# Block-diagonal K and V operands for windowed attention, inside a kernel rewritten around one precomputed order

## The chip, the cores and the metric

The kernel runs on one core of a Trainium2 chip. The metric is device time in microseconds (us) of one execution, as the median of several. On one core an execution is called slow when it is over 1.5% above the fastest of the same kernel; times below are of fast runs unless a sentence says otherwise. "PE" is the tensor engine, "PEld" its weight loads, "DVE" the vector engine, "ACT" the scalar engine, "POOL" GpSimd, and "SP" the engine that here does little else than issue DMAs.

## The reference

Two independent computations share one launch, and their outputs stand side by side.

```python
# (a) S4 convolution: L = 2048 steps, D = 1024 channels, N = 128 states
K = jnp.einsum("dn,dnl,dn->dl", Cc, exp(dt * A * l), dt * Bc).real   # the filter
y = irfft(rfft(u padded to 4096) * rfft(K padded))[:2048] + u * Dskip

# (b) attention, 32 heads of 32, each query sees 8 keys: itself and every
#     second position before it (dilation 2)
q, k, v = x @ wqkv
idx = pos[:, None] - (arange(8) * 2)[None, :]        # masked where negative
o = softmax(q . k[idx] / sqrt(32)) . v[idx]
return concatenate([y, o @ wo], axis=-1)
```

## The kernel before

The first part of the kernel (up to 271 us in its trace) makes Q, K and V by matrix products and, woven in between, the convolution filter with 2048 tiny matmuls. The second part runs the convolution as FFT stages by matmul, and the attention. Even and odd positions are split, so that the dilated window becomes 8 neighbours; queries and keys go in blocks of 32. Four heads of 32 rows share the 128 partitions.

Attention loads whole rows for 256 queries (`ru`) with three DMAs, and multiplies with four packed 32x32 tiles of the array per key block, one for each head:

```python
    def loads(self, ru):
        ...
        nc.sync.dma_start(out=qs[:], in_=self.qv[:, :, q0:q0 + RU])
        nc.sync.dma_start(out=ks[:, :, 32 * f:], in_=self.kv[:, :, q0 - 32 + 32 * f:q0 + RU])
        nc.sync.dma_start(out=vs[:, f:, :], in_=self.Vd[:, b0 - 1 + f:b0 + 8, :])

    # scores of one group of four heads (ct): 9 key blocks x 4 heads
    for b in range(-1, NB):
        ...
        for h in range(4):
            hs = slice(32 * h, 32 * h + 32)
            nc.tensor.matmul(S[hs, o:o + n], lhsT=ks[hs, ct, kb:kb + 32], rhs=qs[hs, ct, qa:qa + n],
                             start=True, stop=True, tile_position=(32 * h, 32 * h), ...)
```

Two generators, convolution and attention, are interleaved by a fixed ratio. The convolution sends its intermediate results (`Zu`, `Zk`, `Zv`) through DRAM to change their layout, and multiplies the two spectra straight from PSUM:

```python
    # step 1, for u and for the filter k
    self.bal.copy(zs[:, 2 * rp:2 * rp + 2, :], pz[:], 1024)
    ...
    nc.sync.dma_start(out=Z[:, n2:n2 + 4, :], in_=zs[64 * b:64 * b + 64])
    # middle
    nc.gpsimd.dma_start(out=t[64 * ri:64 * ri + 64], in_=self.Z[n][hf]...)
    V.tensor_tensor(out=pr[:, x], in0=F[1][:], in1=kf[...], op=ALU.mult)     # F[1] in PSUM, f32

    drive(conv(), 64 + 36 + 16, at.gen(), 80)
```

The softmax here doesn't subtract the row's maximum and nothing guards it: scores larger than these inputs give would overflow.

## Time and profile before

| | before |
|---|---|
| median of 3 runs | 691.88 us (686.53 to 692.02) |
| span of the profiled run | 688.6 us, mean granted PE clock 0.846 |
| PE / DVE / ACT / POOL busy | 70% / 55% / 54% / 15% |
| first part, 0 to 271 us | PE bound from 92 us on |
| second part, 271 to 688.6 us | no engine bound; waits on loads, on order, on instruction supply |

A page of the profile gives busy times over the whole span, then the span in 40 slices (busy tenths of each engine, granted PE clock in tenths, DMA share), the DMA queues, the chain of work that ended last, the costliest groups of instructions, and the DMA issues. The prediction below shows most of what matters. Two lines that it does not show are needed later. They are from the page of the kernel before, the granted clock by slice and the line of the queue that SP fills (packets, MB, share of the 16 DMA engines' time):

```profile
PEclk9997999999999898655885955687997997699979
...
q1 hardware_dynamic: 95376, 88.63, 49.3%
```

The clock falls in the middle of the span, where PE waits; and SP's queue moves 88.63 MB with 95376 packets, 929 bytes each on average.

### The profile page before, as it was taken

How to read it: one execution, taken by the hardware profiler on the slowest of the kernel's cores; microseconds unless marked ns; L12 is line 12 of the kernel's file. 1: busy time of each engine (PE TensorE's matmuls, PEld its weight loads, DVE VectorE, ACT ScalarE, POOL GpSimd, SP SyncE). 2: the span in 40 equal slices, each digit the busy share in tenths (PEclk: the TensorE clock that was granted, in tenths of full speed). 3: DMA queues.
4: the chain of work that ended last, by engine and by line, in shares of the span. 5: the costliest groups of instructions: out<-in, count | busy, mean ns of one | idle time of the engine just before them, and what ended most of it. 6: DMA issues, size and time to landing. Idle time of an engine off the chain costs nothing.

```text
span 688.6 us, 23065 instructions
## 1 busy us (share of the span) xinstructions
PE 484.9 (70%) x10268; PEld 247.5 (36%) x10268; DVE 376.1 (55%) x595; ACT 369.0 (54%) x608; POOL 105.4 (15%) x163
## 2 busy tenths in 40 slices
PE   0284989899999785303775962569788885779866
PEld 0031546556556455102343431224332341223432
DVE  4758878768777802221544431245855862576442
ACT  3585798698798623102554432334646752656441
POOL 5400111010110000000010020000545644350000
PEclk9997999999999898655885955687997997699979
DMA  9980322132231164999585699375997899894685
GB/s 145 258 165 16 93 79 92 59 102 72 79 103 66 54 223 136 255 181 253 136 272 177 199 224 178 91 231 145 328 270 199 243 218 253 220 264 99 185 223 161
DMA packets 103891, 116.19 MB, mean 169 GB/s; under 512 B 46992, under 2 KB 84112, under 8 KB 102128
## 3 DMA queue, kind: packets, MB, share of 16 engines
q1 hardware_dynamic: 95376, 88.63, 49.3%
q0 software_dynamic: 8416, 26.10, 13.9%
q8 instruction: 80, 1.31, 0.8%
q14 instruction: 19, 0.16, 0.1%
HBM read 58.59 MB, written 50.33 MB: 158 GB/s over the span
## 4 chain that ended last, share of the span: by engine, by line
PE 35%; DVE 15%; DMA 15%; ACT 14%; issue 10%; SPq 3%; POOL 0%; ACTq 0%; DVEq 0%
PE cp L579 6%; PE ps L383 6%; DMA Zv<-vs 4%; PE psv L399 4%; DMA big<-Zv 4%; PE cp L627 3%; DVE OR L195 3%; PE O L566 3%; PE S L550 2%; PE pk L239 2%; PE cp L653 2%; DVE OL L224 2%; PE cp L669 2%; DVE OL L223 2%; DMA Kd<-K 2%
## 5 line engine op out<-in xcount | busy, mean ns | idle before, releaser
L383 PE MATMUL ps<-xT,w 128*128 128x512 bf16 x512 | 129.7, 403 | 53.7 <-DMA xT<-in_B_x_dram 32.8
L659 DVE TENSOR_TENSOR pr<-cp,kf 128x1024 bf16<-128x1024 f32 x64 | 75.7, 1219 | 42.7 <-ACT kf L499 33.5
L383 PEld LDWEIGHTS <-w 128*128 128x128 bf16 x512 | 49.1, 102 | 119.1 <-issue 61.9
L550 PE MATMUL S<-qs,ks 32*32 32x40 bf16 (+2 forms) x2304 | 38.9, 185 | 60.3 <-ACT pe L553 20.9
L579 PE MATMUL cp<-wosb,oT 128*128 128x512 bf16 x256 | 62.4, 397 | 4.7 <-ACT zs L499 2.8
L570 ACT ACTIVATE ln<-O 128x256 f32<-128x256 f32 x64 | 24.6, 384 | 73.2 <-PE O L566 66.3
L643 POOL DMA_DIRECT2D zk<-Zk x64 | 38.2, 600 | 164.3 <-PE S L550 82.9
L399 PE MATMUL psv<-wv,xT 128*32 128x256 bf16 x2048 | 62.2, 273 | 0.0
L550 PEld LDWEIGHTS <-ks 32*32 32x32 bf16 x2304 | 27.5, 96 | 93.7 <-issue 72.9
L643 POOL DMA_DIRECT2D zu<-Zu x64 | 38.1, 600 | 138.9 <-PE S L550 117.3
L572 DVE TENSOR_TENSOR oT<-O,ln 128x256 bf16<-128x256 f32 x64 | 27.0, 422 | 54.4 <-ACT ln L571 54.4
L627 PE MATMUL cp<-big,l 128*128 128x512 bf16 x128 | 43.2, 450 | 18.2 <-DMA big<-in_A_u_dram 12.9
L399 PEld LDWEIGHTS <-xT 128*32 128x32 bf16 x2048 | 52.5, 97 | 7.2 <-issue 6.4
L499 ACT CAST vs<-cp 128x1024 bf16<-128x1024 f32 x32 | 32.4, 1012 | 39.8 <-DMA Zv<-vs 26.3
L502 DVE CAST zs<-cp 128x1024 bf16<-128x1024 f32 x36 | 43.0, 1218 | 17.5 <-PE cp L627 17.4
L553 ACT ACTIVATE pe<-S 128x320 bf16<-128x320 f32 x64 | 27.7, 433 | 43.3 <-PE S L550 42.3
L554 DVE TENSOR_TENSOR pm<-pe,mk 128x320 bf16<-128x320 bf16 x64 | 20.3, 320 | 50.8 <-ACT pe L553 32.4
L669 PE MATMUL cp<-pr,m 64*128 64x512 bf16 x256 | 41.2, 423 | 7.7 <-ACT vs L499 5.5
L499 ACT CAST zs<-cp 128x1024 bf16<-128x1024 f32 x28 | 28.0, 1009 | 34.2 <-PE cp L627 22.1
L182 DVE TENSOR_SCALAR PA<-PH 128x1024 int32<-128x1024 int32 (+1 forms) x36 | 27.9, 775 | 27.2 <-ACT TL L186 19.4
L579 PEld LDWEIGHTS <-oT 128*128 128x128 bf16 x256 | 25.2, 102 | 37.2 <-issue 11.8
L653 PE MATMUL cp<-zu,m 128*64 128x512 bf16 x128 | 24.0, 437 | 20.0 <-ACT vs L499 13.2
(105 smaller groups left out, 750.2 us busy)
## 6 DMA issues: line engine op xcount, KB each, us to landing
Zu<-zs SPq DMA_DIRECT2D x32, 256.0 KB, 5.1
Zk<-zs SPq DMA_DIRECT2D x32, 256.0 KB, 5.5
zu<-Zu POOLq DMA_DIRECT2D x64, 128.0 KB, 6.3
zk<-Zk POOLq DMA_DIRECT2D x64, 128.0 KB, 6.1
Zv<-vs SPq DMA_DIRECT2D x64, 128.0 KB, 3.9
big<-Zv SPq DMA_DIRECT2D x16, 512.0 KB, 7.6
w<-in_B_wqkv_dram POOLq DMA_DIRECT2D x16, 256.0 KB, 4.9
QT<-sg SPq DMA_DIRECT2D x16, 256.0 KB, 2.1
```

The costliest lines, as they stand in the source:

```text
L182: V.tensor_scalar(out=PA[:, 0:n, :], in0=PH[:, 0:n, :], scalar1=16384.0, scalar2=None, op0=ALU.add)
L383: nc.tensor.matmul(ps[:, h, :], lhsT=self.w[ct][:, kt, t, :], rhs=self.xT[:, kt, t0:t0 + 512], start=(kt == 0), stop=(kt == 7))
L399: nc.tensor.matmul(ps[32 * h:32 * h + 32, b * 256:b * 256 + 256].rearrange("p (c d) -> p c d", d=32), lhsT=self.xT[:, kt, t0:t0 + 32], rhs ...
L499: self.nc.scalar.copy(out=out, in_=in_)
L502: self.nc.vector.tensor_copy(out=out, in_=in_)
L550: nc.tensor.matmul(S[hs, o:o + n], lhsT=ks[hs, ct, kb:kb + 32], rhs=qs[hs, ct, qa:qa + n], start=True, stop=True, tile_position=(32 * h, 3 ...
L579: nc.tensor.matmul(po[:, h, :], lhsT=oT[:, ct, tt * 128:(tt + 1) * 128], rhs=self.wo[:, ct, h * 512:(h + 1) * 512], start=(ct == 0), stop= ...
L627: nc.tensor.matmul(pz[:, i, :], lhsT=self.l1[:, mt, :], rhs=src[:, rq * 4 + rp * 2 + i, :], start=True, stop=True)
L643: nc.gpsimd.dma_start(out=t[64 * ri:64 * ri + 64], in_=self.Z[n][hf][4 * p + ri:4 * p + 4:2].rearrange("ab n d -> n ab d"))
L653: nc.tensor.matmul(f[64 * ab:64 * ab + 64, ri, :], lhsT=w[:, ab, 64 * ri:64 * ri + 64], rhs=z[:, ab, :], start=True, stop=True, tile_posit ...
L659: V.tensor_tensor(out=pr[:, x], in0=F[1][:], in1=kf[:, x:x + 1, :].to_broadcast([128, 2, 512]), op=ALU.mult)
L669: nc.tensor.matmul(v[:, ab, :], lhsT=w[rs, t, :], rhs=pr[rs, x, y, :], start=(i == 0), stop=(i == 3), tile_position=(64 * ab, 0), skip_gro ...
```

## The change

The title names block-diagonal operands. Instead of four packed 32x32 matmuls, K of four heads stands as four 32x32 blocks on the diagonal of a 128x128 operand whose other elements are zero, and one full-array matmul does all four heads; the same for V. The zeros are written once into three sets of operands. The price is that a load must place each head's blocks separately. The diff is much larger than that, though: nearly the whole kernel is rewritten.

- All work is cut into tasks, and one precomputed order, stored as a table, fixes the sequence on every engine, SP and POOL included. Stage boundaries go.
- DMA transposes of x and of the parameters become plain loads and 176 PE transposes.
- `Zu`, `Zk` and `Kd` no longer go through DRAM; u is reordered inside DRAM by 16 DMAs with runs of 128 B.
- V is made by full-array matmuls. Both spectra are copied to SBUF as bf16 before the product.

```diff
-    def loads(self, ru):
-        nc.sync.dma_start(out=qs[:], in_=self.qv[:, :, q0:q0 + RU])
-        nc.sync.dma_start(out=ks[:, :, 32 * f:], in_=self.kv[...])
-        nc.sync.dma_start(out=vs[:, f:, :], in_=self.Vd[:, b0 - 1 + f:b0 + 8, :])
+        self.kb = [cst.tile([128, 2, 9, 128], BF, name=f"kb{i}") for i in range(3)]
+        self.vb = [cst.tile([128, 9, 2, 128], BF, name=f"vb{i}") for i in range(3)]
+    def load(self, ru, qt, i, st):                      # 32 times: 8 ru x 4 qt
+        nc.sync.dma_start(out=st["q"][:], in_=self.QT[ru][:, 2 * qt:2 * qt + 2, :])
+        for h in range(4):
+            hs = slice(32 * h, 32 * h + 32)
+            nc.sync.dma_start(out=self.kb[i][hs, :, :, hs]..., in_=self.KT_[ru][hs, 2 * qt:2 * qt + 2, :]...)
+        for h in range(4):
+            hs = slice(32 * h, 32 * h + 32)
+            for c in range(2):
+                nc.sync.dma_start(out=self.vb[i][hs, f:, c, hs], in_=self.Vd[hs, b0 - 1 + f:b0 + 8, 64 * qt + 32 * c:64 * qt + 32 * c + 32])
 ...
-                    for h in range(4):
-                        nc.tensor.matmul(S[hs, o:o + n], lhsT=ks[hs, ct, kb:kb + 32], rhs=qs[hs, ct, qa:qa + n], ..., tile_position=(32 * h, 32 * h))
+            nc.tensor.matmul(S[:, o:o + n], lhsT=st["k"][:, ct % 2, kb, :], rhs=st["q"][:, ct % 2, qa:qa + n], ...)
 ...
+            nc.vector.memset(self.kb[i][:], 0.0); nc.vector.memset(self.vb[i][:], 0.0)
 ...
+                    ld = P("SP", 3.2, ... self.load(ru, ct // 2, i, st) ...)     # 3.2: the task list's own figure for a load
 ...
-    drive(conv(), 64 + 36 + 16, at.gen(), 80)
+        seq = plan.order()                               # a table of 1864 entries, decoded from text
+        for t in seq:
+            t.fn(t.pick)
```

## The prediction

> **What bounds the kernel now.** I read the page's engine totals and slices first, then the busy time by stretch, then the waits of the tensor engine, the groups, the chain and the DMA queue's issues.
>
> ```profile
> span 688.6 us, 23065 instructions
> PE 484.9 (70%) x10268; PEld 247.5 (36%) x10268; DVE 376.1 (55%) x595; ACT 369.0 (54%) x608; POOL 105.4 (15%) x163
> ...
> 0.00:27.00 27.00, 0.00 (x0) 0.10 (x1) 13.86 (x29) 14.80 (x23) 12.71 (x20) 1.00 1.04 203
> 27.00:92.00 65.00, 44.94 (x396) 20.85 (x396) 51.58 (x69) 43.92 (x66) 8.43 (x6) 0.92 0.49 109
> 92.00:271.00 179.00, 163.20 (x4226) 100.89 (x4226) 118.26 (x219) 134.10 (x223) 8.21 (x10) 0.96 0.27 89
> 271.00:318.00 47.00, 10.55 (x206) 5.35 (x205) 14.11 (x39) 6.71 (x11) 0.00 (x0) 0.58 1.01 220
> 318.00:490.00 172.00, 114.95 (x2908) 57.58 (x2909) 71.38 (x114) 70.51 (x142) 9.50 (x16) 0.71 0.71 195
> 490.00:640.00 150.00, 118.41 (x1845) 46.83 (x1845) 88.24 (x102) 82.84 (x118) 66.53 (x112) 0.87 0.87 230
> 640.00:688.60 48.60, 32.85 (x688) 15.89 (x686) 18.71 (x27) 16.08 (x31) 0.00 (x0) 0.89 0.67 191
> ```
>
> In each stretch the columns are length, busy PE, weight load, DVE, ACT and POOL, then granted clock, DMA share, GB/s. No engine bounds the whole. Up to 271 us is the first half (QKV projection and generation of the convolution filter), the rest is convolution and attention. Only one stretch, 92 to 271, is bound by PE (163 of 179 us). Before 27 us PE does nothing, from 27 to 92 it is busy 45 of 65; from 271 to 318 DMA is full and PE is all but idle; after that everything is half used, at a reduced clock. The waits and chain say on what:
>
> ```profile
> PE ps L383 <- DMA xT<-in_B_x_dram: 32.8, 8, 27.0
> PE ps L383 <- ACT sg L386: 13.2, 5, 9.9
> ...
> PE S L550 <- ACT pe L553: 20.9, 28, 1.1
> PE S L550 <- issue: 19.9, 7, 6.6
> PE S L550 <- DMA ks<-KT: 19.2, 2, 15.8
> PE cp L653 <- ACT vs L499: 13.2, 9, 4.5
> PE cp L627 <- DMA big<-in_A_u_dram: 12.9, 1, 12.9
> ...
> PE 35%; DVE 15%; DMA 15%; ACT 14%; issue 10%; SPq 3%; POOL 0%; ACTq 0%; DVEq 0%
> ```
>
> The first matmul waits 27 us for the DMA transposes of x. Later the fixed order of the two interleaved generators makes PE stand before scores whose single PSUM buffer is still being read (ACT pe), before loads, and for its own instructions (issue). The chain changes hands everywhere: this is a latency and ordering problem, so a better order can gain much.
>
> ```profile
> L659 DVE TENSOR_TENSOR pr<-cp,kf 128x1024 bf16<-128x1024 f32 x64 | 75.7, 1219 | 42.7 <-ACT kf L499 33.5
> L550 PE MATMUL S<-qs,ks 32*32 32x40 bf16 (+2 forms) x2304 | 38.9, 185 | 60.3 <-ACT pe L553 20.9
> L566 PE MATMUL O<-pm,vs 32*32 32x40 bf16 (+1 forms) x2240 | 29.9, 186 | 8.4 <-issue 8.4
> Zv<-vs SPq DMA_DIRECT2D x64, 128.0 KB, 3.9
> zu<-Zu POOLq DMA_DIRECT2D x64, 128.0 KB, 6.3
> ```
>
> These are the rows that the named part of the change touches, plus the round trip through DRAM that the rest of the diff removes.
>
> **What the Trainium skill says.** (1) "TensorE: Matmul & The Clock Gate", Part 1: an idle window of about 3.4 us takes the array to half clock. The trace agrees: 0.58 granted in 271 to 318, 0.96 where PE is dense. (2) "TensorEngine Tiling (Array Packing)", Instruction Overhead: a matmul costs about 60 cycles however few columns it has. The trace's packed 32x32 matmuls run 32 in 0.37 us, 12 ns each with four tiles at work, that is 46 ns for four; so one full-array matmul of 40 columns should take about what four packed ones did. (3) "DMA: Bandwidth & Descriptors", Specifications: at least 512 B for line rate. The packet records agree: median 18 ns of one DMA engine for 256 B, 27 for 512 B, 47 for 1 KB, 85 for 2 KB, 9 for a 4 B semaphore write; short packets are nearly all fixed cost. (4) "Perfetto Trace Analysis", What "DMA-bound" means: the issuing sequencer can itself be the bound. Here 128-partition DMAs occupied SP 0.32 to 0.39 us (QT, osb), those on 64 partitions 0.45 to 0.57 (Zu, Zv medians 0.60), on 16 or 32 about 0.55 at least (Kd).
>
> **The change part by part.** The diff is far more than its title: nearly all is rewritten, and every engine gets one precomputed order. The durations written in its task list are somebody's model; I take none of them.
>
> *Start.* DMA transposes of six parameters and of x give way to plain loads plus 11 x 16 = 176 PE transposes. The adjacent 128-column shift matmuls of before stand 0.055 us apart warm, 0.107 cold, so 10 to 19 us PE, say 15; and 11 PSUM copies of 2048 elements, about 2 x 1.01 us on ACT each, 22 us shared with DVE. Plain loads of the first 2 MB of x and 1.5 MB parameters at the 300 GB/s or so that the busiest stretches show take some 12 us, so QKV starts near 12 us, not 27 with stutter until 46.
>
> *First half.* PE work: 64 x 1.83 us QK = 117; V as full-array matmuls instead of column-packed, 32 x 1.76 = 56, unchanged; filter matmuls 32 x 0.65 = 21; shift 2; transposes 15; one conv step, 8. Sum 219. ACT had 194 us here and DVE 189, and together get about 20 us more: near 200 each, close behind PE. 12 + 219 + 10 of losses: it ends near 240 instead of 271.
>
> *Convolution.* Zu and Zk no longer go through DRAM: 64 writes and 128 reads of 1 KB packets go, 32768 x 47 ns / 16 = 96 us of all 16 DMA engines, with the POOL issues. Kd goes too. New: 32768 packets of 128 B to reorder u inside DRAM (about 14 ns by interpolation, 29 us, in the first half). The product's 64 x 1.22 us from PSUM (76 us) becomes about half from bf16 in SBUF (an OL product of 2048 bf16 took 1.22 us, so 1024 about 0.65; 42 us) but needs a copy of u, 32 x 1.0 to 1.2 = 35. Near zero on balance.
>
> *Attention.* Matmuls fall from 2304 + 2240 to 576 + 560, PE time by (2) about 64 x 0.42 + 64 x 0.54 = 61 us either way. PE instructions in total fall from 20536 to some 12900, so the issue waits (10% of the chain, while DMA is full) should shrink. Buffers: three sets of loads, scores may use other PSUM rings. Price: each of 32 loads becomes 13 DMAs on SP (1 q, 4 k, 8 v) with 4608 runs of 64 B. At 12 to 16 ns (between the 4 B and 256 B rows) 145000 runs cost 109 to 145 us of all DMA engines.
>
> *Second half, floors.* PE: of 430 us warm in all, 211. ACT + DVE: attention 79 + 47, evacuations of step 1 71, mid copies 107, products 42, output copies 36, filter expansion 18: 400, so 200 each. DMA: the runs 109 to 145, the rest by the packet medians (Zv both ways, filter sends, q, constants, outputs, semaphores) 137: 246 to 282. SP: 416 block loads x 0.40 to 0.55 = 166 to 229, other DMAs about 80: 246 to 309. So the small pieces, not PE, set this half: 270 to 300 with some tail, against 418 before.
>
> Sum: 240 + 280 = 520 us, that is 172 us (25%) less: about 31 from the start and first half, 140 from the second.
>
> **Rivals.** (a) *PE-bound throughout.* If 64 B runs are cheaper than I take them and issue costs 0.3 us, the second half approaches 211 us of PE at 90%: 235 + 5 tail, total 480 to 490. For: the order was optimised with this in view, and the clock will recover. Against: 46992 packets under 512 B already gave full DMA with 120 to 150 GB/s at 290 to 300 us. (b) *SP or DMA becomes the wall.* At 0.55 us an issue or 16 ns a run, with stores queued behind loads on one in-order SP queue, the second half is 320 to 340 and the total 560 to 580. For: Kd issues stretched to 7.5 us when the rings were full. (c) *Nothing gained*, the gain in order eaten by loads: needs a second half above 440 us, where no sum above comes near. (d) *ACT/DVE-bound first half*: with table loads and filter products out of step it stays at 260 to 270, total 540 to 550.
>
> **Range and chances.** The centre 520 lies between (a) and (b); I hold (a) at three in ten, (b) at two to three in ten. Range 485 to 580. To miss the 2% mark the kernel must lose 158 us against the centre: faster 0.97, same 0.02, slower 0.01.
>
> **What would show it.** Right: first QKV matmul before 16 us; the last near 235 to 245; transposes of x gone from the DMA list; score matmuls about 576 at 30 to 60 ns spacing; issue in the chain below 7%; DMA share in the second half above 0.85 with GB/s below before's 200; SP issues of the block loads 0.4 to 0.55 us; PE clock above 0.9. Wrong: DMA share of 0.6 and PE above 90% there (rival a); PE waiting mainly on kb and vb loads and SP never idle (b); QKV ending after 260 (d); or score matmuls above 90 ns apart, which would add 40 us of PE. The weakest number is the cost of a 64 B run, of which the trace of before holds hardly any.

## The result, and the profile after

The kernel after takes 649.24 us (median of 4 runs, 647.49 to 651.81) against 690.08 us (4 runs, 686.53 to 692.02). The ratio is 0.9417, with a 95% interval of 0.9361 to 0.9472; ratios here are the mean time of one kernel's fast runs over that of the other's fast runs of the same rounds, so not quite the ratio of the medians. So it is 5.8% faster, where some 25% had been predicted, and the measured time lies far outside the predicted range.

The first view is the busy time by stretch of the kernel after, cut at the starts and ends of its stages. The columns are as in the prediction: length, then busy time of PE, PEld, DVE, ACT and POOL with the number of instructions, then granted clock, DMA share, GB/s.

```profile
0.00:50.00 50.00, 32.17 (x245) 21.14 (x246) 36.19 (x52) 31.19 (x41) 17.74 (x24) 0.93 0.60 186
50.00:275.00 225.00, 191.94 (x2835) 100.57 (x2834) 179.17 (x341) 169.37 (x268) 1.63 (x3) 0.92 0.50 115
275.00:631.00 356.00, 245.31 (x3020) 144.93 (x3018) 174.32 (x294) 169.72 (x294) 15.58 (x29) 0.80 0.69 135
631.00:650.00 19.00, 11.23 (x45) 4.45 (x43) 1.34 (x2) 5.97 (x6) 0.00 (x0) 0.91 0.58 180
```

The first part now ends at 275 us, not at 240 as predicted and not earlier than before. It does more than before, since some convolution work has moved into it. The second part takes 375 us: 356 with loads in it and 19 of tail. In those 356 us no compute engine and no DMA engine is full: PE 245 at a clock of 0.80, DVE and ACT under half, DMA 0.69. This is what the page before looked like too, so the reader has to ask what is full instead. The queue line, the sums of the chain and its lines by source, from the page of the kernel after, answer:

```profile
q1 hardware_dynamic: 263648, 74.23, 54.5%
...
q8 instruction: 48, 0.79, 0.5%
...
PE 16%; DMA 14%; SPq 14%; issue 13%; ACT 3%; DVE 2%; DVEq 0%; ACTq 0%; POOLq 0%
SPq L681 5%; PE cp L762 5%; SPq L677 4%; DMA kb<-KT 4%; DMA Zv<-vs 3%; DMA big<-Zv 3%; PE cp L879 3%; PE cp L857 2%; DMA out_dram<-yb 2%; PE cp L824 2%; SPq L887 2%; PE cp L923 1%; PE S L690 1%; SPq L913 1%; DMA out_dram<-osb 1%
```

SP's queue ("SPq") went from 3% of the chain before to 14%, and its two largest lines are those of the new loads: 681 (`vb`) and 677 (`kb`). Bytes went down (88.63 to 74.23 MB), packets up by a factor of 2.8. SP is not on the page's list of engine times, since issuing a DMA is not counted as busy. One has to look at its timeline. This is an excerpt of SP's timeline after (start, length, instruction, how many; a length covers all of the row's instructions):

```profile
415.03 4.42 SPq L681 DMA_DIRECT2D vb<-Vt  x7
419.87 0.34 SPq L674 DMA_DIRECT2D qs<-QT  x1
420.26 2.04 SPq L677 DMA_DIRECT2D kb<-KT  x4
422.40 3.93 SPq L681 DMA_DIRECT2D vb<-Vt  x8
```

A row starts less than half a microsecond after the one before it ended, and it goes on like this. Summed from the records, SP issued 554 DMAs between 275 and 631 us. They took 316.1 us themselves and left 540 gaps of under 0.2 us, 31.5 us together, or 0.058 us each. So SP was occupied for 348 of 356 us. In the kernel before, from 271 to 688 us, it was 236 DMAs, 193.7 us, and 213.5 us of true waiting. By line the 316.1 us after are: `vb` 256 x 0.518 = 132.7; `kb` 128 x 0.639 = 81.8; `qs` 32 x 0.508 = 16.3; all the rest 85.3. One load of 13 DMAs thus costs 0.51 + 4 x 0.64 + 8 x 0.52 + 13 x 0.058 = 8.0 us. The kernel's own task list has 3.2 us for it, as the diff shows.

The tile view of the kernel after gives the spread of single issues (count, then shortest/median/longest in ns, first and last start):

```profile
L677 SPq DMA_DIRECT2D kb<-KT x128: 302/496/6207, 278.7 to 617.5; - x128
```

```profile
L681 SPq DMA_DIRECT2D vb<-Vt x256: 303/453/2481, 287.0 to 623.3; - x128
```

The loads of the attention thus run from 279 to 623 us almost without a pause, and everything else follows them. What PE waited for, from the waits of the kernel after (us in total, times, longest):

```profile
PE pk L378 <- issue: 26.4, 10, 4.2
PE S L690 <- DMA kb<-KT: 16.6, 9, 4.2
PE O L705 <- DVE pm L699: 13.5, 5, 5.9
PE cp L705 <- DVE pm L699: 10.0, 5, 4.3
PE cp L923 <- DMA out_dram<-osb: 8.3, 1, 8.3
PE cp L923 <- DMA kb<-KT: 6.3, 1, 6.3
```

All rows but the first are the second part's. No single row of the second part is large. PE's order is fixed, so when the next load is late PE stands, its clock sinks to 0.80, and the work that is left takes longer: 256.5 us busy from 275 to 650, where the same matmuls took 220 us once issues had been moved off SP (E2 below).

The first row belongs to the first part. PE was ready to go on with the filter's 2048 small matmuls (L378), all inputs were there, and it stood ten times, 26.4 us in all. The records say more. Counted over all PE instructions in order, the nine such stops over 2.2 us lie apart by 512, 512, 256, 256, 1024, 512, 512 and 512 instructions: whole multiples of 256. The queue named "instruction" moved 48 packets of 16 KiB, and each of these stops ended 1.2 to 1.6 us after such a packet had come in. The Trainium skill says in "Runtime: NRT & Kernel Launch", section "Instruction fetch mechanics", that instructions come in blocks of 16 KiB, 256 instructions, and that crossing a boundary is mostly hidden. The size agrees. That it is hidden does not agree here: in a run of small matmuls, which stood 9.3 ns apart on average and each bring a weight load along, the blocks came 3.4 to 4.8 us apart, while 128 pairs need only 1.2 us.

The row of the score matmuls (L690) among the costliest groups of the kernel after, to be set beside row L550 in the prediction (operation, operands, shapes and count; busy time and mean ns; idle time of PE before it and what ended most of that):

```profile
L690 PE MATMUL S<-qs,kb 128*128 128x40 bf16 (+2 forms) x441 | 19.9, 184 | 22.5 <-DMA kb<-KT 16.6
```

The count fell from 2304 to 576 (441 here, the other 135 under another tile's name), and its largest wait is no longer for ACT but for `kb`. The product of the two spectra, not shown, fell from 75.7 to 41.3 us, as predicted. Score matmuls on the full array stand 26 ns apart in the median, 29 in the mean; in the packed form of E1 the mean was 7.2 ns, which is 29 for four. The form of the matmul is neutral on PE.

### The profile page after: what moved, and what is told of

The parts are those of the page before. It is cut to its first block, busy times and chain, and to the rows that moved or that the text cites. A ratio compares the mean times of both kernels' runs of the same rounds, so it can differ in the third digit from the quotient of the medians.

```text
span 650.0 us, 15338 instructions
## 1 busy us (share of the span) xinstructions
PE 480.6 (74%) x6140; PEld 271.1 (42%) x6140; DVE 391.0 (60%) x687; ACT 376.3 (58%) x607; POOL 34.9 (5%) x56
## 3 DMA queue, kind: packets, MB, share of 16 engines
q1 hardware_dynamic: 263648, 74.23, 54.5%
## 4 chain that ended last, share of the span: by engine, by line
PE 16%; DMA 14%; SPq 14%; issue 13%; ACT 3%; DVE 2%; DVEq 0%; ACTq 0%; POOLq 0%
SPq L681 5%; PE cp L762 5%; SPq L677 4%; DMA kb<-KT 4%; DMA Zv<-vs 3%; DMA big<-Zv 3%; PE cp L879 3%; PE cp L857 2%; DMA out_dram<-yb 2%; PE cp L824 2%; SPq L887 2%; PE cp L923 1%; PE S L690 1%; SPq L913 1%; DMA out_dram<-osb 1%
## 5 line engine op out<-in xcount | busy, mean ns | idle before, releaser
L618 PE MATMUL ps<-wv,xT 128*128 128x512 bf16 x256 | 65.4, 409 | 6.6 <-DMA wv<-in_B_wqkv_dram 4.1
L824 PE MATMUL cp<-l,big 128*128 128x256 bf16 x256 | 43.4, 318 | 13.2 <-ACT zu L466 5.2
L466 ACT CAST sg<-ps 128x1024 bf16<-128x1024 f32 x38 | 37.9, 1005 | 23.5 <-issue 9.2
L871 DVE TENSOR_TENSOR pr<-uf,kf 128x1024 bf16<-128x1024 bf16 x64 | 41.3, 687 | 4.4 <-ACT uf L466 3.0
L824 PEld LDWEIGHTS <-big 128*128 128x128 bf16 x256 | 35.5, 174 | 19.4 <-issue 14.9
L378 PE MATMUL pk<-OR,OL 128*32 128x21 bf16 x2048 | 22.4, 184 | 27.6 <-issue 26.4
L618 PEld LDWEIGHTS <-xT 128*128 128x128 bf16 x256 | 26.0, 103 | 39.2 <-issue 11.3
L857 PEld LDWEIGHTS <-m 64*64 64x64 bf16 x1024 | 30.3, 123 | 24.5 <-issue 21.5
L690 PEld LDWEIGHTS <-kb 128*128 128x128 bf16 x576 | 21.3, 101 | 36.6 <-issue 24.8
L690 PE MATMUL S<-qs,kb 128*128 128x40 bf16 (+2 forms) x441 | 19.9, 184 | 22.5 <-DMA kb<-KT 16.6
L378 PEld LDWEIGHTS <-OL 128*32 128x32 bf16 x2048 | 20.2, 114 | 33.2 <-issue 32.1
L468 DVE CAST uf<-cp 128x1024 bf16<-128x1024 f32 x21 | 25.7, 1222 | 11.3 <-PE cp L857 11.2
```

The lines of the kernel that those rows point to most:

```text
L378: nc.tensor.matmul(pkv[32 * g:32 * g + 32, q, :], lhsT=OL[:, ri, dh, :, dl], rhs=OR[:, ri, h * DH + dh, :, dl], start=(ri == 0), stop=(ri ...
L466: nc.scalar.copy(out=out, in_=in_)
L618: nc.tensor.matmul(st["ps"][:, b, :], lhsT=self.xT[:, kt, t0:t0 + 128], rhs=self.wv[:, kt, :], start=(kt == 0), stop=(kt == 7))
L690: nc.tensor.matmul(S[:, o:o + n], lhsT=st["k"][:, ct % 2, kb, :], rhs=st["q"][:, ct % 2, qa:qa + n], start=True, stop=True, skip_group_che ...
L824: nc.tensor.matmul(w["pz"][:, i, :], lhsT=src["t"][:, :, 4 * pi + i], rhs=self.l1[:, lk], start=True, stop=True, skip_group_check=True)
L857: nc.tensor.matmul(f[64 * ab:64 * ab + 64, c2, ri, :], lhsT=t[rs, ab, o:o + 64], rhs=z[rs, 4 * p + 2 * ab + zi, :], start=(zi == 0), stop= ...
```

## The experiments

The main theory (A): the second part is set by SP, and what costs is the number of DMAs it has to issue, 13 per load. The rivals: (B) the 64 B runs, that is, the descriptors and the DMA engines' time for them; (C) the full-array matmuls or the clock; for the first part: (P) the stops before the runs of filter matmuls cost their full 26 us, or (Q) the first part is bound by something else beside them. The kernels of one call ran on the same chip. In the first call too few runs of the kernel before were fast for a ratio (one of them, 674.09 us, made most others count as slow), so those four kernels are compared with each other; all their own runs were fast. In the second call (E5 to E8) the record gives ratios but leaves the verdict against the kernel before at "unclear". The calls ran on different chips (12, 7 and 11), and the kernel after was not run again in any of them. What ties them together is the kernel before: its median over all runs was 688.78, 688.85 and 685.96 us in the three calls, and 690.08 beside the kernel after, within 0.6% of each other. Differences between calls of some per cent can therefore be read, smaller ones cannot.

### E1, e1_packed: undo the named part only

The new order and everything else stay. K and V are loaded contiguously, 3 DMAs per load, and the packed matmuls return.

```diff
-        for h in range(4): ... kb[i][hs, :, :, hs] <- KT_[ru][hs, ...]      # 4 DMAs
-        for h in range(4): for c in range(2): ... vb[i][hs, f:, c, hs] <- Vd  # 8 DMAs
+        nc.sync.dma_start(out=st["k"][:], in_=self.KT_[ru][:, 2 * qt:2 * qt + 2, :])
+        nc.sync.dma_start(out=st["v"][:, f:, :], in_=self.Vd[:, b0 - 1 + f:b0 + 8, 64 * qt:64 * qt + 64])
-            nc.tensor.matmul(S[:, o:o + n], lhsT=st["k"][:, ct % 2, kb, :], ...)
+            for h in range(4):
+                nc.tensor.matmul(S[hs, o:o + n], lhsT=st["k"][hs, ...], ..., tile_position=(32 * h, 32 * h))
```

> The title part alone undone inside the changed kernel: K and V are loaded contiguously (3 DMAs a load instead of 13, no 64 B runs) and the heads go in four packed 32x32 matmuls, as before; the precomputed order is unchanged. Theory A (the SP queue's issue bounds the second half: 554 DMAs x 0.63 us = 348 of its 356 us): 320 issues fewer, some 190 us less on SP, so PE and ACT bound the half next, at 250 to 280 us; total 540 to 560 us. Theory B (the 64 B runs on the DMA engines bound it): the same total, since the runs go too. Theory C (the order was computed from wrong durations and PE waits on other engines whatever the loads do): at most 30 us off, 615 or more.

Correct, 555.05 us (551.31 to 557.4). The same kernel, repeated as e11_packed_again, gave 558.93 us (557.66 to 559.64), ratio to the kernel before 0.8143 (0.81 to 0.8187). So the named part of the change costs some 92 us, and all the rest of the diff gains about 130. The busy time of E1's second part:

```profile
275.00:550.00 275.00, 230.38 (x6440) 139.21 (x6467) 169.39 (x289) 175.19 (x299) 15.62 (x29) 0.96 0.70 188
```

PE is busy 84% of it at a clock of 0.96. The sums of the chain on its page have SPq at 1%, where it was 14%:

```profile
PE 27%; DMA 5%; DVE 3%; issue 3%; ACT 3%; SPq 1%; ACTq 0%; DVEq 0%
```

SP issued 239 DMAs for 143.8 us of these 275. That names the part, but not which of its properties: issues, runs and matmul form changed together. The first part still ended at 275 us.

> The packed kernel (title part undone) once more, unchanged, as the yardstick for the other two on this chip: 550 to 560 us.

### E2, e2_poolv: the same DMAs, issued from two queues

Everything is as in the kernel after, but the 256 loads of `vb` are issued from POOL.

```diff
-                nc.sync.dma_start(out=self.vb[i][hs, f:, c, hs], ...)
+                nc.gpsimd.dma_start(out=self.vb[i][hs, f:, c, hs], ...)
```

> The same transfers, but the 256 V block loads are issued from the POOL queue, which is 5% busy. Theory A (SP issue): SP loses 256 x 0.57 us = 146 us of the second half, total 520 to 570 us unless POOL takes over 1 us for each. Theory B (64 B runs): the runs are all still there, time within 2% of 649. Theory C: 630 or more.

Correct, 557.6 us (555.21 to 560.17). The bytes, matmuls and order are those of the kernel after, and 92 us of the 649.24 measured for it before are gone. The busy time of its second part, and the row of the issues on POOL from its groups:

```profile
275.00:550.00 275.00, 219.79 (x3023) 133.90 (x3045) 171.87 (x293) 171.03 (x297) 169.51 (x285) 0.94 0.95 184
```

```profile
L681 POOL DMA_DIRECT2D vb<-Vt x256 | 153.0, 605 | 71.9 <-DVE vb L730 40.5 <-PE cp L712 9.6 <-DMA vb<-Vt 6.4
```

Theory B was expected to leave the time near 649. E2 is not a clean test of it, however, because the 64 B packets changed with the queue. The queue lines of this run (SP's, then POOL's):

```profile
q1 hardware_dynamic: 187872, 69.63, 58.5%
q0 software_dynamic: 11216, 13.85, 12.6%
```

The packets of 64 B fell from 153616 to 81936. The V loads issued on POOL are recorded as 4096 packets of 1024 or 1152 B, which took 32 us of all 16 DMA engines, where the V loads' 71680 packets of 64 B on SP's queue had taken some 49 (estimated: 71680 packets at their mean of 11.0 ns, over 16 engines). What rules B out is E3 and E8 below. The block loads are not free, though: the DMA share is 0.95 here, against 0.70 in E1, which is 0.95 x 275 = 261 us of work. C falls: full-array matmuls with the clock back at 0.94 do the work in 220 us. One POOL issue took 0.605 us, longer than the same issue on SP, but it ran beside SP. The Trainium skill says in "DMA: Bandwidth & Descriptors", section "Issuing engines are not separate DMA queues", that issuing from several engines only saves the sequencer's own time, "which is usually small relative to the DMA itself". Here that saving is all there is, and it is 92 us, for DMAs of 18 KB.

### E3, e3_fewruns: the same issues, few runs (wrong result on purpose)

All 13 DMAs stay, each on the same partitions, but they bring only one or two key blocks instead of nine.

```diff
-            ... out=self.kb[i][hs, :, :, hs]..., in_=self.KT_[ru][hs, 2 * qt:2 * qt + 2, :]...
+            ... out=self.kb[i][hs, :, 1, hs], in_=self.KT_[ru][hs, 2 * qt:2 * qt + 2, 32:64]
-                ... self.vb[i][hs, f:, c, hs], in_=self.Vd[hs, b0 - 1 + f:b0 + 8, ...]
+                ... self.vb[i][hs, 1:3, c, hs], in_=self.Vd[hs, b0:b0 + 2, ...]
```

> Wrong result on purpose: the same 12 K and V DMAs a load, on the same queue, but each carries only one or two key blocks instead of nine (16 thousand runs of 64 B instead of 145 thousand). Theory A (SP issue count): within 3% of 649, down at most by the stretched issues (some 20 us). Theory B (64 B runs): 100 us or so less DMA work, total 540 to 580 us. Theory C: within 2%.

622.54 us (618.29 to 625.1), 27 us less than after, a little more than the 3% that A allowed. Most runs are gone (24576 remain, not the 16 thousand of the expectation, where the kernel after has 145408), and so is a third of the DMA engines' load (share 0.48 from 275 to the end at 623, against 0.69), but only 27 of the 92 us come back. They come back through SP too: from 275 us on its issues took 280.1 us instead of 316.1. `kb` fell from a mean of 0.639 to 0.471 us, `vb` from 0.518 to 0.462. So the runs have a share in the loss by stretching the issues, and the count has the rest. B as the sole cause (540 to 580) is out.

### E8, e8_plus10: the packed kernel with ten useless issues per load

To E1 ten DMAs of 2 KB per load are added, on SP, into tiles that nobody reads. Each load has 13 issues again, while runs, matmuls and data stay those of E1.

```diff
         nc.sync.dma_start(out=st["v"][:, f:, :], in_=...)
+        for x in range(10):
+            idle = self.ld.tile([128, 32], BF, name=f"idle{x}")
+            nc.sync.dma_start(out=idle[32 * (x % 4):32 * (x % 4) + 32, :], in_=self.Vd[...32 partitions, 32 elements])
```

> The packed kernel plus ten useless SP DMAs per load (32 runs of 64 B each, into scratch that nobody reads): 13 issues a load as in the changed kernel, but only 0.3 KB of runs per DMA and packed matmuls. Theory A (issue count): 320 x 0.55 us more on SP, total 610 to 650. Theory B (runs) or the matmul form: within 3% of 555.

Correct, 651.97 us (650.59 to 656.38), ratio 0.9506 (0.9412 to 0.9599). It lies 2 us above the range expected by A. This is the kernel after's time (649.24), made from the fast kernel by nothing but issues. The useless DMAs in the tile view of this run:

```profile
L677 SPq DMA_DIRECT2D idle<-Vt x320: 302/420/9637, 276.5 to 625.8; - x160
```

Their median is 0.42 us, their mean 0.55. They fill SP to 30.1 us of gaps and 317.4 us of issues between 275 and 635 us, as in the kernel after, and the DMA engines are only 0.54 busy. With E2 and E3 this settles A: taking issues off SP gives the time back, taking most runs away while the issues stay gives back only 27 us, and adding issues takes the time away with hardly any runs.

### E6, e6_halfpool: half of the V loads on POOL

```diff
-                nc.sync.dma_start(out=self.vb[i][hs, f:, c, hs], ...)
+                (nc.gpsimd if c else nc.sync).dma_start(out=self.vb[i][hs, f:, c, hs], ...)
```

> Half of the V block loads (128 of 256) from POOL, the rest as in the changed kernel: the dose between 649 (none moved) and 558 (256 moved). Theory A: 128 x 0.57 = 73 us less on SP, so 570 to 585, as long as SP, at 275 us, is still the longest in the second half. Theory B: 640 or more.

Correct, 590.69 us (587.78 to 595.34), ratio 0.8625 (0.852 to 0.873): a little above what was expected. SP issued 424 DMAs for 257.9 us with 24.3 us of short gaps between 275 and 570, 96% of those 295 us. So SP was still full, and the kernel moved with it: 282 us of SP work gave 590, 348 us gave 649. That is 59 us of time for 66 us of SP.

### E10, e10_kdiag: only K block-diagonal

K keeps its 4 DMAs and the full-array score matmuls; V is loaded with one DMA and multiplied in packed form. A load has 6 DMAs.

```diff
-        for h in range(4): for c in range(2): ... vb[i][hs, f:, c, hs] <- Vd       # 8 DMAs
+        nc.sync.dma_start(out=st["v"][:, f:, :], in_=self.Vd[:, b0 - 1 + f:b0 + 8, 64 * qt:64 * qt + 64])
+            for h in range(4):
+                nc.tensor.matmul(O[hs, 0, qa:qa + n], lhsT=st["v"][hs, ...], rhs=pm[hs, o:o + n], ..., tile_position=(32 * h, 32 * h))
```

> Half the title: K block-diagonal and full-array scores, V contiguous and packed: 6 DMAs a load instead of 13. Theory A: 7 x 32 x 0.6 = 134 us less on SP in the second half, about 215 us against a floor of 275 set by the rest: 552 to 570 us, as the packed one. Rival (the SP queue already hurts before it is full, since loads and stores wait behind each other, as with half of the V loads moved): 570 to 590.

Correct, 554.84 us (552.66 to 558.48), ratio 0.8091 (0.8035 to 0.8147), against 558.93 for the packed kernel. SP had 329 DMAs, 223.5 us and 19.7 us of short gaps, in the 265 us from 275 on. Up to here the issues do not cost. It is the fastest correct kernel together with E1 (E9 below leaves work out), and the difference between the two is within their scatter: E1 itself gave 555.05 and 558.93 on two chips.

### E5, e5_poolexp: contiguous loads, operands built on chip by POOL

K and V land contiguously (3 DMAs per load), and POOL copies each head's blocks onto the diagonal.

```diff
+        nc.sync.dma_start(out=ks[:], in_=self.KT_[ru][:, 2 * qt:2 * qt + 2, :])
+        nc.sync.dma_start(out=vs[:, f:, :], in_=self.Vd[...])
+        for h in range(4):
+            nc.gpsimd.tensor_copy(out=self.kb[i][hs, :, :, hs], in_=ks[hs]...)
+        for h in range(4):
+            nc.gpsimd.tensor_copy(out=self.vb[i][hs, f:, :, hs], in_=vs[hs, f:, :]...)
```

> The block-diagonal matmuls stay, but K and V come contiguously (3 DMAs a load) and POOL copies them into the zeroed operands (8 copies a load, 256 in all). Theory A: SP is as free as in the packed kernel (555 us). If the full-array form itself is neutral, 545 to 575; if its fewer PE instructions are worth something, below 550. Rival D: the POOL copies (over 1 us each[...]) or the single landing buffer become the bound: 580 or more.

Correct, 602.61 us (597.52 to 604.73), ratio 0.8765 (0.8669 to 0.8861). The wall moved to another queue, as rival D of the expectation had it. PE's largest wait in this run:

```profile
PE cp L859 <- DMA m<-c_m: 31.2, 11, 5.1
```

`m` is a table for the convolution that POOL loads; its 32 loads now stood behind 256 copies of about 0.66 us (median) on the same in-order engine. The single landing buffer, the other half of rival D, shows as well: SP waited 38.9 us in all for these copies before the next V load. The two were not tested apart.

### E4 and E7: spread the filter matmuls

E4 (e4_pkspaced) is the kernel after with PE's order changed, so that at most 96 filter matmuls follow each other. E7 (e7_packed_spaced) does this to E1, and moves the copies of the displaced products along.

```diff
-        return out
+        return self.spaced(out)     # swaps PE tasks, keeping dependencies and buffer counts, until no run exceeds 96
```

> Only the order of PE tasks in the first half is changed: runs of 256 and 512 small filter matmuls are broken into runs of at most 96 with QKV matmuls between. Theory P (in long runs PE outruns its instruction fetch: 26 us of issue waits in front of them): those waits fall below 8 us and the total by 12 to 20 us, to 630 to 637. Theory Q (the first half is bound by the filter's DVE and ACT work, the waits cost nothing): within 1% of 649.

> The packed kernel with the filter matmuls of the first half broken into runs of at most 96, and this time the ACT or DVE copy that empties each moved QKV unit moved along right behind it. Theory P (issue waits before long runs of small matmuls cost first-half time): PE no longer waits for copies as in the first try, the 25 us of issue waits go, total 535 to 545. Theory Q (DVE and ACT bound the first half): 550 to 575.

Both are correct and both missed: E4 took 665.95 us (662.33 to 668.53), 17 more than after; E7 took 603.68 us (596.64 to 605.56, three fast runs; a fourth, the profiled one, counts as slow with 606.26), some 45 to 49 more than the packed kernel. The stops went, from 26.4 to 2.4 us in E4, but others came in their place. From the waits of PE in E4:

```profile
PE ps L637 <- ACT sg L516: 13.4, 5, 6.0
...
PE ps L668 <- ACT sg L516: 7.3, 4, 2.4
```

The QKV products now came where their PSUM buffers had not yet been copied out, while ACT still followed the order made for the old sequence. In an order that is fixed for all engines at once, moving one engine's tasks undoes the fit of the others. These two kernels therefore say that the stops come from long runs of small matmuls, but nothing on what their absence is worth.

### E9, e9_pkhalf: half of the filter matmuls

To avoid the reordering, E9 takes E1 and leaves out the imaginary half of the filter products. This was meant to give a wrong filter; with these inputs the result stayed within the tolerance.

```diff
-                    for ri in range(2):
+                    for ri in range(1):
                         ... nc.tensor.matmul(pkv[...], lhsT=OL[:, ri, ...], rhs=OR[:, ri, ...], ...)
```

> Wrong result on purpose, on the packed kernel: the filter matmuls of the first half take only the real part, 1024 instead of 2048, so the runs are 64 to 256 long; nothing else moves. The matmuls left out are about 1024 x 9.3 ns = 10 us of PE. Theory P (first half bound by PE, issue waits included): issue waits of 25 us fall to some 5, first half 25 to 30 us shorter, total 525 to 532. Theory Q (DVE and ACT bound the first half): total within 8 us of the yardstick.

549.22 us (543.02 to 550.88), ratio 0.7986 (0.7911 to 0.806), against 558.93 for the full kernel. Some 11 us of matmuls and all 22 us of stops before them were gone, and the last V product of the first part ended at 255.0 instead of 266.6 us. From the waits of PE in E9:

```profile
PE pk L378 <- ACT kraw L466: 15.1, 4, 6.2
PE ps L587 <- ACT sg L466: 5.5, 4, 2.0
```

So about a third of the removed time came back as time, and the rest turned into waits, mostly for ACT. P and Q are both half right: with less for PE to do, the copies on ACT hold the first part back almost as much.

### All kernels

| kernel | DMAs per load on SP | median, us | SP occupied in the second part |
|---|---|---|---|
| before | 3 per 256 queries | 690.08 | 203 of 417 |
| after | 13 | 649.24 | 348 of 356 |
| E8, packed + 10 useless | 13 | 651.97 | 348 of 360 |
| E3, few runs (wrong) | 13 | 622.54 | 311 of 348 |
| E6, half of V on POOL | 9 | 590.69 | 282 of 295 |
| E2, V on POOL | 5 | 557.6 | 207 of 260 |
| E10, K diagonal only | 6 | 554.84 | 243 of 265 |
| E1, packed | 3 | 555.05 and 558.93 | 156 of 275 |
| E5, operands by POOL copies | 3 | 602.61 | (POOL is the wall) |
| E4, after with spread filter | 13 | 665.95 | not compared |
| E7, packed with spread filter | 3 | 603.68 | not compared |
| E9, packed, half the filter | 3 | 549.22 | not compared |

(SP occupied: its issues and the gaps under 0.2 us between them, summed from the records.)

## Why the prediction was wrong

The predicted sum was 240 + 280 = 520 us. Measured were 275 + 375 = 650 for the profiled run. Both terms failed, the second by far more.

**The second half: the SP term, and the chance given to rival (b).** The step that failed reads "SP: 416 block loads x 0.40 to 0.55 = 166 to 229, other DMAs about 80: 246 to 309. So the small pieces, not PE, set this half: 270 to 300 with some tail". The direction was right: the small pieces set it. Three sizes were off, all the same way. First, the 416 block loads took 230.8 us, 0.555 each, just above the top of the span, and the sum was then read from its middle. Second, the space between two issues was not counted; at 0.058 us for each of 540 it is 31.5 us. Third, the tail: with loads arriving until 623 us, the work that depends on the last ones ran until 650, 19 us past the stretch. Put together, 231 + 85 + 32 is 348 us of SP, with 8 us of waiting and 19 of tail: 375. Rival (b) named the right wall, "SP never idle", but without the gaps and the tail it made the second half 320 to 340 us and the total 560 to 580, and it got a chance of "two to three in ten".

With the issues off SP (E2) or cut down (E1, E10), the second part takes 275 to 280 us. That this is the predicted 280 is luck: the 280 came from the SP sum, and in these runs SP is occupied only 156 to 243 us, so something else sets the half there (in E1 PE is busy 84% of it, in E2 the DMA share is 0.95). The other floors were about right. PE was put at 211 us warm and took 220 (E2) and 230 (E1). DMA was put at 246 to 282 and did 0.69 x 356 = 246 in the kernel after, and 261 in E2. ACT and DVE were put at 200 each and took about 170 to 175.

**The DMA runs.** A 64 B run was put at 12 to 16 ns and called the weakest number. It took 11 ns (median; 153616 packets, 105 us of all 16 engines). The guess erred towards caution; the weakest number was not the one that failed. That the DMA share in this half would pass 0.85 was wrong (0.69), since SP did not feed the engines; in E2 it was 0.95. One argument about small packets was misread from the trace before: the 46992 packets under 512 B, held against rival (a), are those of the whole run. Between 290 and 300 us the records have 931 packets of 256 B, which took 1.7 us of all 16 engines, and 128 of 8 KB, which took 7.7.

**The first half: "12 + 219 + 10 of losses".** The start was right: the first V matmul came at 13.6 us, where 12 had been put. The work was right: PE was busy 220 us from there to 275 (224 from the start), against 219. The failed term is "10 of losses". After 13.6 us PE stood idle for 41 us: 26.4 us of stops before long runs of filter matmuls, 8 us until 50 us, mostly for x, and 7 us for the rest, mostly for copies on ACT. 13.6 + 220 + 41 is 275. The prediction had counted PE instructions, found fewer of them, and concluded that waits for instructions would shrink to under 7% of the chain; they were 13%. The total did shrink, from 20536 to 12280, but the stops come in long runs of small matmuls (E4 removed them by breaking the runs), and the new order bundles these in runs of 256 to 512. How much of the 35 us these stops alone cost is not settled: two attempts to spread them disturbed the fixed order (E4, E7), and E9 gave 11.6 us in the first part for some 33 us of PE time. Rival (d), ACT and DVE close behind, was right in kind, though the 275 us lie above its "260 to 270" for this half.

**The rest.** The product came out at 41.3 us (42 predicted). DMA transposes are gone from the list. Full-array score matmuls stood 26 ns apart, below the predicted 30 to 60, and are neutral beside packed ones. The granted clock was to pass 0.9 and was 0.80 in the second part, which goes with PE's waiting: with the wall gone it is 0.94 to 0.96 (E1, E2). Of E1's remaining distance to 520, 35 us are thus the first half.

One thing is argued, not shown. The order carries a cost of 3.2 us for a load of 13 DMAs, a quarter of a microsecond each, and of 0.15 us for a `Zv` store of two. Measured were 8.0 us and 1.4. An order made with such costs sees no wall on SP and has no reason to avoid issues. That the model hid the loss fits the numbers, but no run here makes a new order from other costs.

## What to carry to other kernels

Count DMA issues as work of an engine: number of DMAs on a queue times the measured issue time plus the gap after each, set against the length of the stage, before weighing bytes and descriptor sizes. A layout that saves matmul instructions but cuts one load into a dozen can move the bound to the issuing queue, where busy times of engines and DMA share show nothing full; look at the issuing engine's timeline. When all engines follow one frozen order, moving a task on one engine is not a local change, so test a suspected wait by removing its work or its cause, not by rearranging.

## What the Trainium skill lacked or had wrong

- "DMA: Bandwidth & Descriptors", section "Issuing engines are not separate DMA queues": it calls the issue time usually small and gives no figure for it on SP (the page's only one stands among its trn3 figures, for "previous generations"). Measured on SP: single issues from 0.30 us, medians of 0.45 to 0.50 for 32 partitions with 64 B runs, 0.60 for 64 partitions, and 0.058 us between two; under load the means rise to 0.52 to 0.69. For the same 18 KB DMA a POOL issue took 0.61 us. Issues alone made 92 us of 649 here.
- "Perfetto Trace Analysis", section "What "DMA-bound" means": it names the solid issuing sequencer as a bound, which E2 and E8 confirm, but there says that large descriptors are what matters. Taking most of the small runs away gave back 27 us (E3), while fewer issues (E1) or a second queue (E2), which the page's section "DMA Optimizations" does advise, gave 92.
- "Runtime: NRT & Kernel Launch", section "Instruction fetch mechanics": it has 16 KiB blocks as mostly hidden. In runs of small matmuls, 9.3 ns apart with their weight loads, PE stood up to 4.2 us at the boundary, 26.4 us in ten stops, and blocks came 3.4 to 4.8 us apart.
- No page gives the time that one DMA engine takes for a short packet (the 10.5 ns in "DMA: Bandwidth & Descriptors", section "Bandwidth", divide a whole small DMA by its packets). Measured on one engine, out of SP's queue: 11 ns (median) for 64 B, 13 ns for 128 B. The prediction put 12 to 16 for 64 B.
- "DMA: Bandwidth & Descriptors": it does not compare, for this chip, how a load is cut into packets by the queue that it is issued from. The V loads with 64 B runs were 64 B packets on SP's queue and 1024 or 1152 B packets on POOL's (E2).
